# Seven products in place of eight in the first feed-forward product of the last four token blocks

## The chip, the cores and the metric

One core of a Trainium2 chip. The core has five engines with an instruction stream each: PE (TensorE, the matmuls; its weight loads are listed apart as PEld), DVE (VectorE), ACT (ScalarE), POOL (GpSimd) and SP (SyncE, which issues the DMAs here). The metric is the device time of one execution in microseconds; the median of several runs counts.

## The reference

Linear attention with positive random features, whose output goes straight into a feed-forward layer.

```python
# q, k, v: (8 batches, 8 heads, 576 positions, 64); omega: (128, 64)
def phi(x):                          # x is scaled by 64 ** -0.25 before
    h = einsum('bhsd,md->bhsm', x, omega) - sum(x * x, -1, keepdims=True) / 2
    return exp(h - max(h, -1)) / sqrt(128)
num = phi(q) @ (phi(k).T @ v)
den = phi(q) @ sum(phi(k), over positions) + 1e-6
x = (num / den)                      # as (4608 tokens, 512)
h = x @ w_in                         # w_in (512, 2048)
out = gelu(h) @ w_out                # w_out (2048, 512), gelu with erf
```

The matrices `w_in` and `w_out` come as 64-bit floats, which the kernel takes apart itself as 32-bit words. All else is 32-bit.

## The kernel before

**Tiles.** The 4608 tokens are cut into 13 blocks (`TBS`): blocks 0 and 1 of 256 tokens, 2 to 11 of 384, 12 of 256. The 2048 hidden features are cut into 16 chunks of 128. The attention is cut into 32 units: unit k is batch k // 4 and the head pair j = k % 4. Heads 2j and 2j+1 are the 128 rows of x with number j, so a block needs the units of all four j of its batches. Units 0 to 7 run in plain 32-bit arithmetic (`unit_plain`), the others in parts (`split_pre`, `exps_op`, `split_post`). The names at work: `pair`, `shared`, `proj`, `proj_q` (features), `exps` (exponential of a whole unit, one instruction of 2304 columns), `kv` and `kv_split` (features of k times v), `q_trans`, `num`/`num_plain` (numerator and denominator), `den`, `rcp`, `div` (division, which writes x).

**Precision.** From block 1 on a matmul's two operands are each split into a high and a low 16-bit float, after scaling by a power of two, and three products are added in PSUM: high by high, low by high, high by low. So `mm1(n, c, p)` computes a chunk c of h, transposed (128 features by the block's tokens), in 12 matmuls: four pieces of 128 rows of x, three products each, in three steps p. `gelu` works in place in the PSUM bank, `g_high` (ACT) writes the high part, `g_low` (DVE) the low part, and `mm2` multiplies both with the chunk of `w_out` and adds over the chunks in a bank `acc` for every 128 tokens. In block 12 the last 128 tokens go in two halves of 256 columns. `block_high` and `block_low` split x itself, once per block and row piece.

**PSUM.** Eight banks in three rings: `at` (3, the attention), `h` (2, first product), `acc` (3, second product).

**The start.** The weights arrive in 16 pieces (`w_load`), are converted (`w_hi`, `w_lo`, `w_shift`, `w_sign`, `w_round`), their maximum is found (`w_abs` on ACT, L401; `w_max` on DVE), and from it comes the scale for the splitting (`w_high`, `w_low`). Meanwhile units 0 to 7 run, and block 0 in 32-bit arithmetic.

**Order.** The program is not written in the order in which it runs. Every piece of work is an `op` with its engine, an estimated cost, what it reads and writes, and a due time. `Planner.run` simulates the engines and hands out, on each engine, the ready op with the earliest due time. The due times come from tables: `STARTS` (one number a block), `UDUE` (one a division), `OFF` (an offset for each function), and the numbers in `X`. The order on each engine is then fixed in the program. `block(n)` lists the ops of a block, `block_prep` its scales and the splitting of x; `xs_place` says where x of a block lies in SBUF, `batch_v` loads v of a batch.

Of the kernel before, what the change touches and what calls it, by code (L numbers as in the profile page):

```python
# [19 lines left out]
P = 128  # L20
# [12 lines left out]
STARTS = (286.9, 834.1, 550.56, 94.36, 152.04, 442.97, 960.6, 1406.49, 1456.39, 594.17, 474.25, 1641.87, 2052.18, 1177.77)  # L33
UDUE = (-331.2, 545.76, 564.47, 521.85, -788.34, -416.41, -477.91, -798.59, -502.63, -176.28, 509.12, -321.38, 447.22, 1250.34,
# [16 lines left out]
PORT = {'w_shift', 'w_sign', 'w_low', 'q_shift', 'q_max2', 'q_max4', 'q_low', 'v_b', 'k_low', 'kv_d', 'block_low', 'split_om'}
# [170 lines left out]
def favor_attention_ffn(ctx: ExitStack, tc: tile.TileContext, qT, kT, v, omT, w_in, w_out, out):  # L222
# [39 lines left out]
    vt = [cp.tile([P, NV, D + 1], F32, name=f"vt{i}") for i in range(2)]  # L262
# [21 lines left out]
    mp, dp, late, G = [], [], [], {}  # L284
    bufs = dict(at=3, h=2, acc=3, nm=2, cm=2, ct=2, cg=2, zr=2, km=2, kvz=1, qh=1, kvz2=1, qh2=1, dt=1, rt=1, rc=2, mx=1, nq=1, mc=1, kvs=1,
                vsc=2, bs=4, be=2, xs=4, raw=2, r=2 if X['xm'] else 3, lo=2, qt=2, ql=2 if X['qm'] else 4, kvh=1, kvl=1, xh=8, xl=8, g=3, gh=3, gl=3, o=2)
    for k, b in bufs.items():
# [4 lines left out]
                 vsc=(P, 2), bs=(P, 6), be=(32, 1), xs=(P, T), raw=(P, 2048), r=(P, 2 * HS if X['xm'] else HS), lo=(P, 2, M), qt=(P, QW, HS), ql=(P, QW, HS),  # L292
                 kvh=(P, 2, P), kvl=(P, 2, P), xh=(P, T), xl=(P, T), g=(P, T), gh=(P, T), gl=(P, T), o=(P, DM))
    kinds = dict(raw=I32, r=F32R, ql=F32R, kvh=F32R, kvl=F32R, xh=F16, xl=F16, gh=F16, gl=F16)
    pools = dict(raw=dp, r=late, lo=late, qt=late, ql=late, kvh=late, kvl=late, xh=mp, xl=mp, g=mp, gh=mp, gl=mp, o=mp)

    def alloc(name, k):
        if name in ('at', 'h', 'acc'):
            G[k] = pp.tile([P, 512], F32, tag=name, name=name, bufs=bufs[name])
            return  # L300
        if name in ('qh2', 'kvz2'):
            G[k] = qh2 if name == 'qh2' else kvz2
            return
# [197 lines left out]
    for b in range(B):  # L501
        for j in range(NJ):
# [5 lines left out]
            u.v = vt[u.k % 2] if u.kp else vst[:, b % 2, j]  # L508
            u.vk = ('vt', u.k % 2) if u.kp else ('vst', b % 2, j)
# [25 lines left out]
    def load_vst(b):  # L535
        nc.sync.dma_start(vst[:, b % 2].rearrange("p j n d -> p j (n d)"), v[b].rearrange("j p n d -> p j (n d)"))
# [120 lines left out]
    xk, xplace = [0], {}  # L657

    def xs_place(n, j):
        if (n, j) not in xplace:  # L660
            if n < 2:
                xplace[n, j] = (xa[:, j, T0[n]:T0[n + 1]], ('xa', n, j))
            elif n == 2:
                xplace[n, j] = (None, ('xs', n, j))
            else:
                k = NKK + xk[0] % (NF - NKK)
                xk[0] += 1
                xplace[n, j] = (w32f[:, 1, k, 0:T], ('xw', k))
# [16 lines left out]
    started = set()  # L685

    def finish_unit(u, half):
        ps = xs_pieces(u.b, half)
        keys, new = [], []
        for n, c0, c1, r0 in ps:  # L690
            k = xs_place(n, u.j)[1]
            if n == 2 and (n, u.j) not in started:
                new.append(('xs', k))
            else:
                keys.append(k)
            started.add((n, u.j))
        pn = [('pn', u, half, a) for a in range(2)]
        return ps, keys, new, pn

    def out_ops(u, half):  # L700
        ps, keys, new, pn = finish_unit(u, half)
# [5 lines left out]
           new=[(ring, k) for k in pn] + new)  # L707
# [4 lines left out]
        op('DVE', c, div, u, half, due=(2, 2 * u.k + half, 0.0, 0.0), r=pn + [('rt', u, half)], w=keys + [k for _, k in new])  # L712
# [51 lines left out]
    def x_high(u, x):  # L764
        a, b = XR[x]
        nc.scalar.copy(G['r', u, x][:, 0:b - a], xf[:, a:b])  # L766

# [172 lines left out]
    def batch_v(b):  # L940
        us = units[b * NJ:(b + 1) * NJ]
        op('SP', 0, load_vst, b, w=[u.vk for u in us], size=1311e3)
        for u in us:
            op('DVE', 0.8, v_max, u, r=[u.vk], w=[('vm', b)])
        chain(b, 0)
        op('POOL', 0.8, v_scales, b, r=[('exp', b, 0)], new=[('vsc', ('vsc', b))])
        op('ACT', 0.3, v_spread, b, w=[('vsc', b)])

    def split_pre(u):
# [5 lines left out]
        for i in range(NK + 4):  # L955
# [27 lines left out]
        op('DVE', 1.33, q_shift, u, r=[nq], w=qe)  # L983
# [123 lines left out]
    def block_prep(n):  # L1107
# [8 lines left out]
        op('POOL', 0.21, block_out, n, r=[('bs', n), ('wsc', 0)], w=[('bo', n)])  # L1116
        t = TB[n]
# [4 lines left out]
    def ffn_first(n, c):  # L1122
        t = TB[n]
        k = 'F' if n >= N32 else 'F0'
        if n < N32:
# [4 lines left out]
            op('ACT', 0.1 + t / 1000, gelu, n, c, r=[('h', n, c)], new=[('g', ('g', n, c))], tab='g', kind=k)  # L1130
# [22 lines left out]

    def p2():
# [34 lines left out]
    for win in (1, 0):  # L1189
# [6 lines left out]
       w=[('w32', 0, c) for c in range(NF)] + [('e2',)] + [(x, 1, t) for x, n in (('et', NT), ('eq', 4)) for t in range(n)] + [('vst', a, j) for a in range(2) for j in range(NJ)])  # L1196
    op(None, 0, nothing, w=[('w32', 1, c) for c in range(NKK)] + ['kk'] + [('kk', g) for g in range(len(KG))])
    for c in range(NKK, NF):
        op(None, 0, nothing, w=[('w32', 1, c), ('xw', c)])
    done_u = NJ  # L1200
    for n in range(1, NBLK):
        b1 = (T0[n + 1] - 1) // S
        while done_u < (b1 + 1) * NJ:
            u = units[done_u]
            if u.j == 0 and not u.kp:
                batch_v(u.b)
# [12 lines left out]
            if us[-1].j == NJ - 1:  # L1219
                chain(u.b, 1)  # L1220
# [45 lines left out]
```

## Time and profile before

| | us |
|---|---|
| runs, median (lowest to highest of 3) | 991.94 (991.08 to 991.99) |
| span of the profiled execution | 989.5 |
| PE, 0 to 100 us: busy | 83.8 |
| PE, 100 to 150 us: busy | 50.0 of 50 |
| last matmul of the attention (L632) | 850.2 |

The page gives the span of the profiled execution, from its first to its last instruction, and no time of its own for what lies around it; the median of the runs stands 2.4 us above the span. The view by stretch gives the busy time of each engine between two moments. A row of a group reads: line, engine, operation, written tile <- read tiles, shape, count | busy time in us, mean time of one in ns | idle time of the engine before it, and who ended it. A row in order of time reads: start, duration, engine, line, operation, and in brackets the idle time before it. A matmul's recorded time includes its way through the array, during which the next one already streams; its pace is read from the starts.

### The profile page before, as it was taken

How to read it: one execution, taken by the hardware profiler on the slowest of the kernel's cores; microseconds unless marked ns; L12 is line 12 of the kernel's file. 1: busy time of each engine (PE TensorE's matmuls, PEld its weight loads, DVE VectorE, ACT ScalarE, POOL GpSimd, SP SyncE). 2: the span in 40 equal slices, each digit the busy share in tenths (PEclk: the TensorE clock that was granted, in tenths of full speed). 3: DMA queues.
4: the chain of work that ended last, by engine and by line, in shares of the span. 5: the costliest groups of instructions: out<-in, count | busy, mean ns of one | idle time of the engine just before them, and what ended most of it. 6: DMA issues, size and time to landing. Idle time of an engine off the chain costs nothing.

```text
span 989.5 us, 17528 instructions
## 1 busy us (share of the span) xinstructions
PE 966.3 (98%) x5996; PEld 603.3 (61%) x5996; DVE 727.5 (74%) x1947; ACT 734.8 (74%) x1515; POOL 354.2 (36%) x552
## 2 busy tenths in 40 slices
PE   7978999999999999999999999999999999999998
PEld 6666666666656566565656666566655556555576
DVE  4987888888989788888988799878775577421111
ACT  6977859788889869788798878978785677542233
POOL 2233334445347327444453535543431422100000
PEclk7978999999999999999999999999999999999999
DMA  8755322422122032013211132121211100000000
GB/s 254 231 182 160 122 83 70 154 71 62 65 80 73 26 109 73 25 55 100 77 49 60 46 102 81 49 61 45 49 31 51 49 1 33 1 22 12 1 33 22
DMA packets 45992, 70.92 MB, mean 72 GB/s; under 512 B 13392, under 2 KB 21968, under 8 KB 45904
## 3 DMA queue, kind: packets, MB, share of 16 engines
q1 hardware_dynamic: 45904, 69.81, 23.9%
q8 instruction: 48, 0.79, 0.4%
q14 instruction: 40, 0.33, 0.1%
HBM read 60.36 MB, written 9.44 MB: 71 GB/s over the span
## 4 chain that ended last, share of the span: by engine, by line
PE 78%; DVE 11%; ACT 6%; DMA 1%; issue 1%; POOL 1%; SPq 1%; ACTq 0%; DVEq 0%; POOLq 0%
PE h L1058 31%; PE acc L1082 10%; PE acc L1084 9%; PE acc L1083 9%; PE h L1053 3%; PE at L632 3%; PE at L779 2%; PE acc L1079 2%; PE at L801 2%; PE at L880 2%; PE at L575 2%; DVE xl L1047 1%; DVE gl L1074 1%; DMA vt<-in_v 1%; DVE mx L806 1%
## 5 line engine op out<-in xcount | busy, mean ns | idle before, releaser
L771 POOL TENSOR_TENSOR r<-xt,r 64x256 fp32r<-64x256 f32 (+2 forms) x216 | 173.5, 821 | 243.4 <-ACT r L766 163.5
L1058 PE MATMUL h<-xh,wih 128*128 128x384 f16 (+1 forms) x768 | 243.6, 317 | 2.9 <-DVE gl L1074 2.6
L1058 PE MATMUL h<-xl,wih 128*128 128x384 f16 (+1 forms) x768 | 243.8, 317 | 0.0
L1058 PE MATMUL h<-xh,wil 128*128 128x384 f16 (+1 forms) x768 | 243.6, 317 | 0.0
L1082 PE MATMUL acc<-woh,gh 128*128 128x512 f16 (+1 forms) x544 | 205.3, 377 | 0.0
L1084 PE MATMUL acc<-wol,gh 128*128 128x512 f16 (+1 forms) x544 | 204.5, 376 | 0.0
L1083 PE MATMUL acc<-woh,gl 128*128 128x512 f16 (+1 forms) x544 | 204.5, 376 | 0.0
L1074 DVE SCALAR_TENSOR_TENSOR gl<-h,bs,gh 128x384 f16<-128x384 f32 (+1 forms) x192 | 112.5, 589 | 120.4 <-ACT gh L1070 118.9
L1058 PEld LDWEIGHTS <-wih 128*128 128x128 f16 x1536 | 147.1, 98 | 86.0 <-issue 0.7
L1066 ACT ACTIVATE h<-h,bs 128x384 f32<-128x384 f32 (+1 forms) x192 | 102.9, 536 | 92.4 <-PE h L1058 91.0
L1070 ACT ACTIVATE gh<-h,bs 128x384 f16<-128x384 f32 (+1 forms) x192 | 107.5, 562 | 68.8 <-PE acc L1084 56.7
L1058 PEld LDWEIGHTS <-wil 128*128 128x128 f16 x768 | 75.0, 98 | 50.1 <-issue 7.2
L1084 PEld LDWEIGHTS <-gh 128*128 128x128 f16 x560 | 54.8, 98 | 62.6
L766 ACT CAST r<-xt 128x256 fp32r<-128x256 f32 (+2 forms) x216 | 82.7, 409 | 12.4 <-PE at L801 3.4
L1082 PEld LDWEIGHTS <-gh 128*128 128x128 f16 x560 | 54.5, 97 | 48.3 <-issue 0.2
L1083 PEld LDWEIGHTS <-gl 128*128 128x128 f16 x560 | 55.0, 98 | 43.2 <-issue 0.3
L683 DVE TENSOR_TENSOR w<-at,rt 64x128 f32<-64x128 f32 (+6 forms) x168 | 54.6, 325 | 3.7
L779 PE MATMUL at<-om,r 128*128 128x256 f32 x216 | 53.8, 337 | 0.0
L394 POOL TENSOR_TENSOR w<-w 128x1024 int32<-128x1024 int32 x12 | 28.7, 2388 | 65.7 <-DVE w L391 42.0
L643 ACT ACTIVATE dt<-at,vsc 64x288 f32<-64x288 f32 x96 | 47.6, 496 | 4.5 <-PE at L632 2.0
L801 PE MATMUL at<-r,om 128*128 128x288 f32 x192 | 47.4, 337 | 0.0
L648 DVE STREAM_TRANSPOSE rt<-dt 128x288 f32<-128x288 f32 x64 | 30.3, 474 | 21.1 <-ACT dt L643 17.2
(213 smaller groups left out, 1770.7 us busy)
## 6 DMA issues: line engine op xcount, KB each, us to landing
xt<-in_kT SPq DMA_DIRECT2D x56, 288.0 KB, 3.9
xt<-in_qT SPq DMA_DIRECT2D x56, 288.0 KB, 3.8
out_x<-o SPq DMA_DIRECT2D x35, 256.0 KB, 2.0
raw<-in_w_in SPq DMA_DIRECT2D x16, 512.0 KB, 6.3
raw<-in_w_out SPq DMA_DIRECT2D x16, 512.0 KB, 4.5
w<-in_v SPq DMA_DIRECT2D x6, 1280.0 KB, 6.2
vt<-in_v SPq DMA_DIRECT2D x8, 320.0 KB, 5.0
out_x<-o SPq DMA_DIRECT2D x2, 128.0 KB, 1.9
```

The costliest lines, as they stand in the source:

```text
L683: nc.vector.tensor_tensor(x[r, c0:c1], ps[r, r0:r1], rt[r, r0:r1], op=ALU.mult)
L766: nc.scalar.copy(G['r', u, x][:, 0:b - a], xf[:, a:b])
L771: nc.gpsimd.tensor_tensor(r, xf[D:, a:b], r, op=ALU.subtract)
L779: nc.tensor.matmul(o[:, t], r[:, t * P:(t + 1) * P], om, start=True, stop=True)
L801: nc.tensor.matmul(G['pp', u, NK + g][:, 0:HS], om[:, i], xr_part(u, NK + g), start=(i == 0), stop=(i == 1))
L1058: nc.tensor.matmul(h[:, 0:t], w, (G['xh', n, j], G['xh', n, j], G['xl', n, j])[k][:, 0:t], start=(i == 0), stop=(i == 3 * NJ - 1))
L1066: nc.scalar.activation(h, h, AF.Gelu, scale=G['bs', n][:, 2:3])
L1070: nc.scalar.activation(G['gh', n, c][:, 0:t], G['h', n, c][:, 0:t], AF.Copy, scale=G['bs', n][:, 3:4])
L1074: nc.vector.scalar_tensor_tensor(G['gl', n, c][:, 0:t], G['h', n, c][:, 0:t], G['bs', n][:, 3:4], G['gh', n, c][:, 0:t], op0=ALU.mult, op1 ...
L1082: nc.tensor.matmul(acc, gh[:, s], woh[:, c, c0:c1], start=(c == 0), stop=False)
L1083: nc.tensor.matmul(acc, gl[:, s], woh[:, c, c0:c1], start=False, stop=False)
L1084: nc.tensor.matmul(acc, gh[:, s], wol[:, c, c0:c1], start=False, stop=(c == NF - 1))
```

## The change

For blocks 9 to 12 (`is_w`) the first product is done by Strassen's method in Winograd's form. `w_in` transposed is cut into four quarters: chunks 0 to 7 and 8 to 15, rows j = 0, 1 and j = 2, 3 of x. x of a block is cut the same way by rows, and by halves of the tokens. With A for the weights and B for x:

- sums of weights, once: S0 = A21 + A22, S1 = S0 - A11, S2 = A11 - A21, S3 = A12 - S1 (`s_sum`, on POOL; for chunks 0 and 1 later and from the 16-bit parts, `s_sum2`), each split into high and low part (`s_high`, `s_low`);
- sums of x, once per block: T1 = B12 - B11, T2 = B22 - T1, T3 = B22 - B12, T4 = B21 - T2 (`b_sum`, on POOL); the seven operands are split by `b_high`, `b_low`;
- two chunks of each half (a group, `q` = 0 to 3) make seven products of 12 matmuls (`w_prod`), on 192 columns (128 in block 12): P1 = A11 B11, P5 = S0 T1, P6 = S1 T2, P2 = A12 B21, P7 = S2 T3, P3 = S3 B22, P4 = A22 T4.

They share three banks. W collects P1 + P6, then P7, then P4. After P1 ACT copies W into V (`w_seed`), to which P2 is added. After P5, which goes to U, ACT copies U into SBUF as s (`w_snap`). After P6 DVE writes W + s into U (`c_sum`), to which P3 is added; after P7 DVE writes W + s into s. V, U, W and s are then the four quarters of h; `c_gelu`, `c_high` and `c_low` treat each of them, and `w_mm2` is the second product as before. W and U come from the rings `h` or `at`, V from `h`.

Besides: `TOP` is 12 in place of 13; the tables `STARTS`, `UDUE`, `OFF` and several numbers of `X` are new; x lies in eight pairs of row pieces (`pair_at`), the copy of k in parts (`kk`) in the buffers of v; v is loaded unit by unit (`load_vst(u)`); tiles `gh` and `gl` are twice as long and also serve block 0.

```diff
-TOP = 13
+TOP = 12
...
-STARTS = (286.9, 834.1, 550.56, 94.36, 152.04, 442.97, 960.6, 1406.49, 1456.39, 594.17, 474.25, 1641.87, 2052.18, 1177.77)
+STARTS = (-608.76, -310.19, 1013.97, 411.45, 613.3, 691.46, 1509.94, 850.35, 1239.92, 423.8, 1230.35, 1650.1, 1806.11,
...
-    def load_vst(b):
+    def load_vst(u):
+        nc.sync.dma_start(u.v, v[u.b, u.j])
...
+    WHICH = ((1, 0, 0), (5, 3, 3), (6, 2, 2), (2, 1, 1), (7, 4, 4), (3, 6, 6), (4, 5, 5))
+    GP = 2
+
+    def is_w(n):
+        return n >= X['n0']
...
+    def s_sum(c, k):
+        a11, a12, a21, a22 = s_src(c)
+        if k % 2 == 0:
+            x, y, o = (a21, a22, ALU.add) if k == 0 else (a11, a21, ALU.subtract)
+        else:
+            x, y, o = (s_tmp(c, 0), a11, ALU.subtract) if k == 1 else (a12, s_tmp(c, 1), ALU.subtract)
+        nc.gpsimd.tensor_tensor(s_tmp(c, k), x, y, op=o)
...
+    def b_sum(n, i):
+        x, y = {3: (7, 0), 2: (6, 3), 4: (6, 7), 5: (1, 2)}[i]
+        nc.gpsimd.tensor_tensor(b_src(n, i), b_src(n, x), b_src(n, y), op=ALU.subtract)
...
+    BANK = {1: 'W', 6: 'W', 7: 'W', 4: 'W', 2: 'V', 5: 'U', 3: 'U'}
+
+    def w_prod(n, q, p, i, first, last):
+        h, b = TB[n] // 2, G[BANK[p], n, q]
+        xh, xl = b_tile(n, i, 0), b_tile(n, i, 1)
+        k = 0
+        for g in range(GP):
+            for kt in range(2):
+                ah, al = a_side(p, GP * q + g, kt)
+                for w, x in ((ah, xh), (al, xh), (ah, xl)):
+                    nc.tensor.matmul(b[:, g * h:(g + 1) * h], w, x[:, kt], start=first and k == 0, stop=last and k == 6 * GP - 1, skip_group_check=True)
+                    k += 1
...
+    def w_snap(n, q):
+        nc.scalar.copy(flat(n, ('s', n, q)), flat(n, ('U', n, q)))
+
+    def w_seed(n, q):
+        nc.scalar.copy(flat(n, ('V', n, q)), flat(n, ('W', n, q)))
+
+    def c_sum(n, q, to):
+        nc.vector.tensor_tensor(flat(n, to), flat(n, ('W', n, q)), flat(n, ('s', n, q)), op=ALU.add)
...
+    def wino_second(n, q):
+        NI, h = TB[n] // P, TB[n] // 2
+        order = ((0, 0), (1, 2), (1, 0), (1, 1), (0, 1), (0, 2)) if NI == 3 else ((0, 0), (1, 0), (1, 1), (0, 1))
```

The tables move instructions on every engine. Three places follow as the order of the built programs shows them, with the engine, the line and the tiles (numbers are buffers).

ACT at the start, around the exponentials of unit 4 (`et` to `et`, 2304 columns). Before; L401 is `w_abs`, L382 and L385 the conversion of weights, L637 `den`:

```order
L385 ACTIVATE w32_71<-raw_507 128x1024
L401 ACTIVATE w32_71,wmax_75<-w32_71 128x1024 x2
L637 ACTIVATE dt_659<-acc_635 128x288
L401 ACTIVATE w32_71,wmax_75<-w32_71 128x1024 x2
L637 ACTIVATE dt_676<-acc_626 128x288
L382 ACTIVATE raw_618<-raw_618 128x1024
L568 ACTIVATE et_82<-et_82 128x2304
```

and with the change, where the same functions are L408, L424, L660, L405 and L591:

```order
L408 ACTIVATE w32_71<-raw_502 128x1024
L591 ACTIVATE et_81<-et_81 128x2304
L424 ACTIVATE w32_71,wmax_74<-w32_71 128x1024
L660 ACTIVATE dt_671<-at_650 128x288
L424 ACTIVATE w32_71,wmax_74<-w32_71 128x1024
L405 ACTIVATE raw_633<-raw_633 128x1024
```

The exponentials now follow the conversion of piece 5 at once; three of the four maxima and the conversion of piece 6 stand behind them.

DVE in the last group of block 12. Before, the low parts of the last chunks follow one another (L1074):

```order
L1074 SCALAR_TENSOR_TENSOR gl_11725<-h_11677,bs_10692,gh_11719 128x256
L1074 SCALAR_TENSOR_TENSOR gl_11763<-h_11714,bs_10692,gh_11758 128x256
L1074 SCALAR_TENSOR_TENSOR gl_11779<-h_11731,bs_10692,gh_11773 128x256
L1074 SCALAR_TENSOR_TENSOR gl_11817<-h_11768,bs_10692,gh_11812 128x256
L1074 SCALAR_TENSOR_TENSOR gl_11830<-h_11785,bs_10692,gh_11825 128x256
```

and with the change (L1307 is `c_sum`, L1328 `c_low`; h_12422 is W, at_12441 is U, h_12439 is V, and s lies in wil):

```order
L1307 TENSOR_TENSOR at_12441<-h_12422,wil_68 128x256
L1328 SCALAR_TENSOR_TENSOR gl_12513<-h_12439,bs_11089,gh_12499 128x2x128
L1307 TENSOR_TENSOR wil_68<-h_12422,wil_68 128x256
L1328 SCALAR_TENSOR_TENSOR gl_12513<-at_12441,bs_11089,gh_12499 128x2x128
L1328 SCALAR_TENSOR_TENSOR gl_12562<-wil_68,bs_11089,gh_12555 128x2x128
L1328 SCALAR_TENSOR_TENSOR gl_12562<-h_12422,bs_11089,gh_12555 128x2x128
```

Two sums of banks stand between the four low parts of a group, and PE waits for each of them before its next product into the bank.

PE at the last product of the program. Before, the last matmul of chunk 15's `mm1` and what follows:

```order
L1058 MATMUL h_11785<-xl_10932,wih_67 128x256
L1082 LDWEIGHTS gh_11719
L1082 MATMUL acc_11479<-woh_69,gh_11719 128x512
L1083 LDWEIGHTS gl_11725
L1083 MATMUL acc_11479<-woh_69,gl_11725 128x512
```

and with the change the last matmul of P4 and the second product (L1392 to L1394) of the first quarter (gh_12499):

```order
L1294 MATMUL h_12422<-xl_11970,wih_67 128x128
L1392 LDWEIGHTS gh_12499
L1392 MATMUL acc_12108<-woh_69,gh_12499 128x512
L1393 LDWEIGHTS gl_12513
L1393 MATMUL acc_12108<-woh_69,gl_12513 128x512
```

Before, 45 matmuls of five chunks follow the last first product, 36 of them of earlier chunks; now 36 matmuls follow, and the six with gh_12499 stand ahead of the first that needs P4 (with gh_12555).

More of the change, by code (lines that the diff above doesn't have):

```diff
@@ L683, in div @@
                 nc.vector.tensor_tensor(x[r, c0:c1], ps[r, r0:r1], rt[r, r0:r1], op=ALU.mult)
-    started = set()
     def finish_unit(u, half):
         ps = xs_pieces(u.b, half)
[L689 to L698, printed above, removed]
+        return ps, [xs_place(n, u.j)[1] for n, _, _, _ in ps], [('pn', u, half, a) for a in range(2)]
     def out_ops(u, half):
-        ps, keys, new, pn = finish_unit(u, half)
+        ps, keys, pn = finish_unit(u, half)
         qs = (half,) if X['qm'] else (half, 2 + half)
@@ L982, in split_pre @@
         op('POOL', 0.23, q_max6, u, w=[nq])
[L983 removed]
+        if X['qs']:
+            op('POOL', 2.14, q_shift_p, u, r=[nq], w=qe)
+        else:
+            op('DVE', 1.33, q_shift, u, r=[nq], w=qe)
     def exps_op(us):
@@ new lines, in s_scale, with s_high, s_low, sums_of_weights @@
+    def s_scale(c):
+        return 1.0 if c < 2 else wsc[:, 1, 1:2]
+    def s_high(c, k):
+        nc.scalar.activation(s_place(c, k)[0], s_tmp(c, k), AF.Copy, scale=s_scale(c))
+    def s_low(c, k):
+        h, l = s_place(c, k)
+        nc.vector.scalar_tensor_tensor(l, s_tmp(c, k), s_scale(c), h, op0=ALU.mult, op1=ALU.subtract)
+    def sums_of_weights(c):
+        ks = [('w32', 1, c), ('w32', 1, c + NF // 2)]
+        parts = [(x, 1, c + y) for x in ('wh', 'w') for y in (0, NF // 2)]
+        for k in range(4):
+            op('POOL', 0.62 if c > 1 else 0.62 * (3, 2)[k % 2], s_sum if c > 1 else s_sum2, c, k, r=(ks if c > 1 else parts) + ['w0f'] + ([('st', c, k // 2)] if k % 2 else []),
+                   new=[('tx', ('st', c, k))])
+        op(None, 0, nothing, w=ks + [('sw', c)])
+        for k in range(4):
+            op('ACT', 0.4, s_high, c, k, r=[('st', c, k), ('sw', c), ('wsc', 1)], w=[('swh', c, k)], kind='W')
+            op('DVE', 0.42, s_low, c, k, r=[('st', c, k), ('sw', c), ('wsc', 1), ('swh', c, k)], w=[('swl', c, k)], kind='W')
@@ L1154, in p2, with w_mm2 @@
+    def w_mm2(n, q, a, g, i, c0, c1, begin, end):
+        acc, c = G['acc', n, i, c0][:, 0:c1 - c0], chunks(q, a)[g]
+        gh, gl = (G[x, n, q, a][:, g * TB[n] + i * P:g * TB[n] + (i + 1) * P] for x in ('gh', 'gl'))
+        nc.tensor.matmul(acc, gh, woh[:, c, c0:c1], start=begin, stop=False)
+        nc.tensor.matmul(acc, gl, woh[:, c, c0:c1], start=False, stop=False)
+        nc.tensor.matmul(acc, gh, wol[:, c, c0:c1], start=False, stop=end)
+    acc_begun = set()
+    WR = X['wr']
     def p2():
@@ L1205, in favor_attention_ffn @@
             if u.j == 0 and not u.kp:
+                if u.k == X['kvp']:
+                    op(None, 0, nothing, w=[('vt', 0), ('vt', 1), 'kk'] + [('kk', g) for g in range(len(KG))])
                 batch_v(u.b)
```

271 lines of the change are left out of this document (221 added, 50 removed), and 8 rows, old and new, of the table UDUE.

## The prediction

> **What bounds the kernel now.** I read first the page of the profile: the span, the busy times, and the row of PE in 40 slices.
>
> ```profile
> span 989.5 us, 17528 instructions
> ...
> PE 966.3 (98%) x5996; PEld 603.3 (61%) x5996; DVE 727.5 (74%) x1947; ACT 734.8 (74%) x1515; POOL 354.2 (36%) x552
> ...
> PE   7978999999999999999999999999999999999998
> ...
> PEclk7978999999999999999999999999999999999999
> ```
>
> TensorE is busy from the fifth slice to the end, at the full granted clock; only the first 100 us have holes. Second, the busy times by stretch (length, then busy time of PE, PEld, DVE, ACT, POOL), third the list of waits of PE.
>
> ```profile
> 0.00:100.00 100.00, 83.83 (x594) 63.41 (x595) 74.95 (x169) 77.00 (x168) 30.31 (x32) 0.86 0.70 208
> 150.00:850.00 700.00, 697.39 (x4318) 426.40 (x4318) 581.12 (x1650) 571.84 (x1201) 306.29 (x506) 1.00 0.21 62
> 850.00:947.00 97.00, 96.91 (x538) 52.51 (x538) 21.57 (x41) 35.63 (x67) 0.23 (x1) 1.00 0.03 9
> ```
>
> ```profile
> PE at L575 <- ACT et L568: 8.3, 2, 5.8
> PE at L613 <- ACT et L559: 4.0, 1, 4.0
> PE h L1058 <- DVE gl L1074: 2.6, 8, 0.6
> ```
>
> From 150 to 850 us PE idles 700 - 697.39 = 2.6 us, from 850 to 947 us 0.1 us. Of the visible waits 12.3 us lie in two lines of the attention at the start. A busy share alone would not do, since a matmul's recorded time overlaps the next one's; so, fourth, the starts of matmuls in the order of time (start, duration, engine, line, operation).
>
> ```profile
> 902.13 0.33 PE L1058 MATMUL h<-xh,wih 128*128 128x384 f16 x1
> ...
> 906.03 0.38 PE L1082 MATMUL acc<-woh,gh 128*128 128x512 f16 x1
> ...
> 909.91 0.33 PE L1058 MATMUL h<-xh,wih 128*128 128x384 f16 x1
> ```
>
> ```profile
> 960.60 0.27 PE L1058 MATMUL h<-xh,wih 128*128 128x256 f16 x1
> ...
> 963.22 0.38 PE L1082 MATMUL acc<-woh,gh 128*128 128x512 f16 x1
> ```
>
> Between 902.13 and 906.03 stand 24 matmuls of 384 columns: 3.90/24 = 162.5 ns from start to start. Between 906.03 and 909.91 stand 18 of 512: 215.6 ns. Between 960.60 and 963.22 stand 24 of 256: 109.2 ns. Each further 128 columns cost 53.2 ns, so a matmul costs about 2.7 ns + 0.416 ns a column, with a weight load for every one. The stream is without gaps: **after the start the time is the number of streamed columns**, and a column removed there is worth 0.416 ns.
>
> **The change part by part.** *Products.* A block of 384 tokens now has 16 chunks x 12 = 192 matmuls of 384 columns in its first product, 192 x 162.5 ns = 31.20 us. Four groups x seven products x 12 = 336 matmuls of 192 columns take their place; at 2.7 + 80 = 82.6 ns (estimate from the line above) that is 27.75 us, 3.45 us less. The block of 256: 192 x 109.2 ns = 20.97 us against 336 of 128 columns at 55.9 ns = 18.78 us, 2.19 us less. Three blocks and one: 3 x 3.45 + 2.19 = **12.5 us off PE**. The matmuls of the second product keep number and shape (48 groups of three in each of the four blocks).
>
> The 55.9 ns is new ground: no long run of such short matmuls is in the trace. The nearest row is the split of k and v, runs of four with 65, 129, 65 and 129 columns:
>
> ```profile
> 205.86 0.34 PE L880 MATMUL at<-vb,w 128*128 128x65 f16 x4
> 206.03 0.33 PE L1058 MATMUL h<-xh,wih 128*128 128x384 f16 x1
> ```
>
> Four matmuls with four weight loads in 0.17 us; the line gives 4 x 2.7 + 388 x 0.416 = 172 ns. So the load does not set the pace even at 65 columns, in a run of four. From the other side, the shortest pace kept up over 24 is the 109.2 ns above. I take 55.9, nearest to the run of short ones, and keep 109.2 for a rival.
>
> On this point the Trainium skill (TensorE: Matmul & The Clock Gate, "Back-to-back issue gap") speaks against the change: in a sustained stream of weight load and matmul it gives about 81 ns per matmul of 128 columns, where the columns alone would take 56. By it the last block's products cost 336 x 25.1 ns = 8.4 us more, and the sum below would be 988.0. The same sentence gives 131 ns for 512 columns, where the rows above show 215.6; no run here shows its figure for 128.
>
> *Work added off PE.* It has these rows as prices (group, count, busy time, mean ns):
>
> ```profile
> L1070 ACT ACTIVATE gh<-h,bs 128x256 f16<-128x256 f32 x32 | 15.2, 474 | 14.9 <-PE at L1084 9.8 <-PE acc L1084 4.8
> L1066 ACT ACTIVATE h<-h,bs 128x256 f32<-128x256 f32 x32 | 14.3, 448 | 16.0 <-PE h L1058 15.9
> L1066 ACT ACTIVATE h<-h,bs 128x384 f32<-128x384 f32 x160 | 88.5, 553 | 76.5 <-PE h L1058 75.2 <-DVE w L683 0.4
> L1043 ACT ACTIVATE xh<-w,bs 128x384 f16<-128x384 f32 x36 | 20.0, 604 | 0.7 <-DVE w L683 0.5
> L1074 DVE SCALAR_TENSOR_TENSOR gl<-h,bs,gh 128x384 f16<-128x384 f32 x160 | 97.2, 611 | 84.3 <-ACT gh L1070 83.0
> L1074 DVE SCALAR_TENSOR_TENSOR gl<-h,bs,gh 128x256 f16<-128x256 f32 x32 | 15.4, 480 | 36.1 <-ACT gh L1070 35.9
> L1047 DVE SCALAR_TENSOR_TENSOR xl<-w,bs,xh 128x384 f16<-128x384 f32 x36 | 23.7, 697 | 2.1 <-POOL bs L309 1.2 <-ACT xh L1043 0.8
> L771 POOL TENSOR_TENSOR r<-xt,r 64x256 fp32r<-64x256 f32 x96 | 74.3, 789 | 140.1 <-ACT r L766 90.2 <-issue 23.7 <-PE at L779 11.9
> ```
>
> ACT gets 32 high parts of weight sums (32 x 0.474 = 15.2 us), 32 copies of banks (24 x 0.553 + 8 x 0.474 = 17.1) and 12 more operands (9 x 0.604 + 3 x 0.474 = 6.9): 39 us. DVE gets 32 low parts (15.4), 32 sums of banks (24 x 0.611 + 8 x 0.480 = 18.5) and 12 operands (9 x 0.697 + 3 x 0.480 = 7.7): 42 us. POOL gets 60 sums; at 0.789 us for 256 columns the 44 of the weights cost 35 us and the 16 of up to 384 at most 16 x 1.18 = 19, against 700 - 306 = 394 us idle. What must fit before 850 us, where the attention still runs, is the weight sums and two blocks, some 29 us of DVE and 27 of ACT; the second row by stretch shows 700 - 581.12 = 119 us idle on DVE and 128 on ACT there, while PE waited 2.6 us in all. I cost it at nothing: it fills idle time beside a PE that has its own work. Without that cover it would be up to 29 us. The loads of v come in 24 pieces instead of 6, which adds 18 issues to a queue that nothing waited for.
>
> *Waits added.* A group's seven products share three banks, and between them stand hand-offs: ACT copies the first product into a second bank and the fifth out of the third, DVE adds twice. The waiting PE instruction would have the rest of the stream behind it. The order puts at least one whole product (12 x 82.6 = 0.99 us) between a sum's source and its user, mostly a product and six matmuls of the second product (2.3 us); a hand-off needs PE's result (about 0.2 us after the last start, since a recorded matmul of 256 columns lasts 0.27 us and the next starts after 0.11) and one 0.48 to 0.61 us operation, 0.8 us if the engine is free. The present chain of three operations per chunk waited eight times, 2.6 us in all 192 chunks, at most 0.6 us. Bounds: 0, and 0.35 us at each of the 32 sums, 11.2 us. I take 1.7, near the present rate. **Tail:** after the last product stand six matmuls that do not need it (6 x 0.2156 = 1.29 us), where 36 did after the last chunk's first product; the chain to be hidden is 0.2 us, gelu 0.45, high part 0.47 and low part 0.48 with hops, about 1.7 us, and one more matmul (0.22) needs only the high part. That leaves 0.2 us, with the copy queue ahead 0.5. Hand-offs and tail: +2.2.
>
> *Order at the start.* The same instructions run in the first 150 us, in another order. The largest wait of PE stands there (start, duration, and in brackets the idle time before):
>
> ```profile
> 52.74 1.19 PE L623 MATMUL h<-w 128*64 128x288 f32 x8
> 59.73 4.21 PE L575 MATMUL at<-vt,et 128*128 128x65 f32 x18 [5.79 <-ACT et L568]
> ```
>
> ```profile
> 55.20 1.06 ACT L401 ACTIVATE w<-w 128x1024 f32<-128x1024 f32 x1 [1.21 <-POOL w L394]
> 56.17 0.19 ACT L401 ACTIVATION_READ_ACCUMULATOR w<-w 128x1 f32 x1
> 56.26 0.39 ACT L637 ACTIVATE dt<-acc 128x288 f32<-128x288 f32 x1
> 56.55 1.12 ACT L382 ACTIVATE raw<-raw 128x1024 f32<-128x1024 f32 x1
> 57.55 2.12 ACT L568 ACTIVATE et<-et 128x2304 f32<-128x2304 f32 x1
> ```
>
> The exponentials of unit 4 stood behind four maxima of weights (about 1.0 us each, one of them waiting 1.21 us for POOL) and a conversion; the new order puts them ahead of all but one of these, three to five us earlier, and those of unit 5 (the other 2.5 us of the 8.3) ahead of the preparation of block 1. What is late next is the division of unit 3, which now has unit 4's and 5's work ahead of it on DVE. Bounds: all 8.3 us won, or as much as the longest wait, 5.8 us, lost elsewhere in the same 100 us. I take -2.0, nearer to the gain since the longest wait's cause is moved.
>
> **The sum** is made on the profiled span, 989.5 us, and what lies around it; the median of the runs shown, 991.94 us, stands 2.4 us above the span, and I leave that as it is. 991.9 - 12.5 + 2.2 - 2.0 = **979.6 us**.
>
> **The rivals.** (a) *The start wins both waits*: -8.3 in place of -2.0, 973.3 us. For it: the two causes are moved; against it: the decode of the weights behind them remains. (b) *The start loses* 5.8 us: 991.9 - 12.5 + 2.2 + 5.8 = 987.4. (c) *A new wait takes the saving's place*: every one of the 32 sums stops PE for 0.35 us, with DVE still full of attention: 991.9 - 12.5 + 11.2 + 0.5 = 991.1, no change. Against it: two of the four blocks run after 850 us, where DVE is busy 22 of 97 us. (d) *The other side: pairs of weight load and matmul have a floor c of their own* in long runs, which the queue hides in runs of four. It acts in the 1344 matmuls of the products; the loss is 336 x (c - 55.9) ns from 56 on, and 1008 x (c - 82.6) ns more from 83 on. It eats the 12.5 us at c = 85, and at 90 ns it is 19 us: 998.6 us, slower. The rows bound c by 43 ns (the run of four) and 109 ns. (e) *The same floor at 80 ns*: only the last block pays, 336 x 24.1 = 8.1 us: 987.7. The 81 ns of the Trainium skill is this case.
>
> **How the numbers follow.** The forecast's own case, between 975 and 985, has 0.56; (a) 0.12, (b) 0.10, (c) 0.08, (d) 0.06, (e) 0.08. Predicted is 979.6. The range takes in (a), (b) and (e) and leaves out (c) and (d), 0.14: 972 to 989. Faster or slower count from 0.2% (2 us), about what a measurement of this kernel can tell from no change: faster 0.56 + 0.12 + 0.10 + 0.08 = 0.86, same 0.08, slower 0.06.
>
> **What would show it.** The product line of blocks 9 to 11 starting every 82 to 83 ns, that of block 12 every 56; at 80 or more in the last, (d) or (e). PE's waits on the two bank sums and copies under 2 us in all; 10 or more is (c). PE idle in the first 100 us at 14 us in place of 16.2. PE idle from 150 to 850 us still near 3 us; if it is 10 or more, the added work of DVE and ACT had no cover. The prediction is wrong if the stage from 150 us on does not shrink by 10 to 13 us.

## The result, and the profile after

The changed kernel takes 984.68 us (median of 4 runs, 984.07 to 985.51) where the kernel before took 991.51 (4 runs, 991.03 to 991.99): ratio 0.9932, 95% interval 0.9918 to 0.9946, so 6.8 us faster. Forecast were 979.6 us, in a range of 972 to 989, and a gain of 12.3.

The page of the changed kernel, with the rows that were shown of before:

```profile
span 982.9 us, 18957 instructions
...
PE 951.7 (97%) x6572; PEld 625.3 (64%) x6572; DVE 768.7 (78%) x2023; ACT 764.7 (78%) x1591; POOL 419.5 (43%) x612
...
PE   7988999899999999999999999999999999999998
...
PEclk7999999999999999999999999999999999999999
```

PE is busy 14.6 us less than before while the span is only 6.6 us shorter; the difference, 8.0 us, is new idle time. The row of tenths is too coarse for it. The busy times by stretch (length, then busy time of PE, PEld, DVE, ACT, POOL, then granted clock) show the place; the first row is of the kernel before, the others of the changed one:

```profile
150.00:400.00 250.00, 249.36 (x1582) 156.51 (x1582) 220.70 (x638) 213.70 (x459) 119.67 (x191) 1.00 0.27 77
```

```profile
0.00:100.00 100.00, 85.31 (x620) 61.66 (x621) 79.89 (x177) 83.98 (x178) 35.43 (x33) 0.93 0.70 212
150.00:400.00 250.00, 240.33 (x1499) 149.68 (x1498) 232.24 (x643) 216.77 (x474) 161.22 (x232) 1.00 0.26 74
150.00:850.00 700.00, 686.90 (x4487) 435.44 (x4486) 597.85 (x1666) 580.37 (x1226) 355.86 (x541) 1.00 0.21 61
850.00:947.00 97.00, 97.00 (x823) 68.86 (x821) 36.50 (x67) 49.08 (x96) 9.20 (x21) 1.00 0.05 17
```

From 150 to 850 us PE idles 13.1 us where it idled 2.6, and 9.7 of them lie between 150 and 400 us, where no product of the new kind has begun; before it was 0.6 there. The list of PE's waits in the changed kernel (total, times, longest) names the line:

```profile
PE h L1081 <- DVE gl L1097: 7.6, 10, 1.7
...
PE at L793 <- POOL r L785: 2.0, 2, 1.8
...
PE h L1294 <- DVE at L1307: 0.7, 1, 0.7
```

The ordinary first products (L1081, `mm1`) wait for a bank `h` that `g_low` (L1097) has to read empty. One such wait in the order of time, with DVE's rows, then POOL's, then PE's (start, duration, in brackets the idle time before):

```profile
185.10 2.33 DVE L1232 SCALAR_TENSOR_TENSOR w<-w,wsc 128x256 f16<-128x256 f32 x1
187.35 0.47 DVE L818 STREAM_TRANSPOSE et<-at 128x288 f32<-128x288 f32 x1
187.86 0.45 DVE L820 TENSOR_REDUCE mx<-et 128x9 f32<-128x288 f32 x1
188.23 0.48 DVE L1097 SCALAR_TENSOR_TENSOR gl<-h,bs,gh 128x256 f16<-128x256 f32 x1
```

```profile
184.84 2.31 POOL L811 TENSOR_TENSOR et<-et,nm 128x1152 f32<-128x1152 f32 x1
```

```profile
186.67 0.38 PE L1107 MATMUL acc<-wol,gh 128*128 128x512 f16 x1
188.76 0.27 PE L1081 MATMUL h<-xh,wih 128*128 128x256 f16 x1 [1.71 <-DVE gl L1097]
```

L1232 is `s_low`, the low part of a sum of weights. It takes 2.33 us and ends 0.28 us after POOL's shift of the features (`k_shift`, L811); three instructions later comes the `g_low` for which PE has stood still 1.71 us. Groups of these sums (busy time, mean ns): two of `s_low` on DVE, and the largest of `s_sum` on POOL:

```profile
L1232 DVE SCALAR_TENSOR_TENSOR w<-w,wsc 128x256 f16<-128x256 f32 x18 | 12.5, 706 | 0.0
L1232 DVE SCALAR_TENSOR_TENSOR w<-xa,wsc,w 128x256 f16<-128x256 f32 x6 | 5.8, 964 | 0.0
L1206 POOL TENSOR_TENSOR w<-w 128x256 f32<-128x256 f32 x18 | 14.2, 797 | 9.6 <-DVE w L1232 8.4 <-DVE vexp L938 0.6
```

The forecast had priced a low part at 0.48 us from a row whose source lies in PSUM; 24 of the 32 take 0.76 us on the mean (18.3 us).

### The profile page after: what moved, and what is told of

Its sections match the earlier page's. It is cut to its first block, busy times and chain, and to the rows that moved or that the text cites. A ratio compares the mean times of both kernels' runs of the same rounds, so it can differ in the third digit from the quotient of the medians.

```text
span 982.9 us, 18957 instructions
## 1 busy us (share of the span) xinstructions
PE 951.7 (97%) x6572; PEld 625.3 (64%) x6572; DVE 768.7 (78%) x2023; ACT 764.7 (78%) x1591; POOL 419.5 (43%) x612
## 4 chain that ended last, share of the span: by engine, by line
PE 68%; DVE 18%; ACT 5%; POOL 3%; issue 2%; DMA 1%; SPq 1%; ACTq 0%; POOLq 0%
PE h L1081 16%; PE h L1294 5%; PE acc L1105 5%; PE acc L1107 5%; PE acc L1106 5%; PE at L1294 5%; PE acc L1393 4%; PE acc L1394 4%; PE acc L1392 4%; PE acc L1102 3%; PE at L655 3%; PE h L1076 2%; DVE gl L1097 2%; PE at L793 2%; PE at L897 2%
## 5 line engine op out<-in xcount | busy, mean ns | idle before, releaser
L785 POOL TENSOR_TENSOR r<-xt,r 64x288 fp32r<-64x288 f32 (+2 forms) x216 | 178.2, 843 | 147.0 <-ACT r L776 107.1
L1081 PE MATMUL h<-xh,wih 128*128 128x384 f16 (+1 forms) x512 | 163.7, 320 | 8.3 <-DVE gl L1097 7.6
L1081 PE MATMUL h<-xl,wih 128*128 128x384 f16 (+1 forms) x512 | 163.7, 320 | 0.0
L1081 PE MATMUL h<-xh,wil 128*128 128x384 f16 (+1 forms) x512 | 163.7, 320 | 0.0
L1105 PE MATMUL acc<-woh,gh 128*128 128x512 f16 x368 | 140.2, 381 | 0.0
L1107 PE MATMUL acc<-wol,gh 128*128 128x512 f16 x368 | 139.5, 379 | 0.0
L1106 PE MATMUL acc<-woh,gl 128*128 128x512 f16 x368 | 139.5, 379 | 0.0
L1081 PEld LDWEIGHTS <-wih 128*128 128x128 f16 x1024 | 97.6, 98 | 55.2 <-issue 0.2
L1097 DVE SCALAR_TENSOR_TENSOR gl<-h,bs,gh 128x384 f16<-128x384 f32 (+1 forms) x128 | 75.6, 590 | 24.9 <-ACT gh L1093 23.5
L1093 ACT ACTIVATE gh<-h,bs 128x384 f16<-128x384 f32 (+1 forms) x128 | 72.3, 566 | 13.1 <-PE acc L1107 9.8
L1081 PEld LDWEIGHTS <-wil 128*128 128x128 f16 x512 | 50.0, 98 | 39.2 <-issue 11.8
L1393 PE MATMUL acc<-woh,gl 128*128 128x512 f16 (+1 forms) x192 | 69.4, 361 | 0.1
L1392 PE MATMUL acc<-woh,gh 128*128 128x512 f16 (+1 forms) x192 | 69.4, 362 | 0.0
L1394 PE MATMUL acc<-wol,gh 128*128 128x512 f16 (+1 forms) x192 | 69.4, 361 | 0.0
```

The costliest lines, as they stand in the source:

```text
L785: nc.gpsimd.tensor_tensor(r, xf[D:, a:b], r, op=ALU.subtract)
L1081: nc.tensor.matmul(h[:, 0:t], w, (G['xh', n, j], G['xh', n, j], G['xl', n, j])[k][:, 0:t], start=(i == 0), stop=(i == 3 * NJ - 1))
L1097: nc.vector.scalar_tensor_tensor(G['gl', n, c][:, 0:t], G['h', n, c][:, 0:t], G['bs', n][:, 3:4], G['gh', n, c][:, 0:t], op0=ALU.mult, op1 ...
L1105: nc.tensor.matmul(acc, gh[:, s], woh[:, c, c0:c1], start=(c == 0), stop=False)
L1106: nc.tensor.matmul(acc, gl[:, s], woh[:, c, c0:c1], start=False, stop=False)
L1107: nc.tensor.matmul(acc, gh[:, s], wol[:, c, c0:c1], start=False, stop=(c == NF - 1))
```

## The experiments

All runs stand beside runs of the kernel before on the same chip, whose median was 990.97 to 991.32 us in the four groups. "Against after" is the difference of medians to a1_after, the changed kernel run again (984.40); e1 to e4 ran as one group, x1, e7, e5 and e6 as the next, a1, f1 and f2 as the third, x2 alone. Since most rows are so compared across groups, a difference under 1 us is not read.

| run | what differs | median us (lowest to highest) | ratio to before, 95% | against after | PE idle 150-400 / 400-700 us |
|---|---|---|---|---|---|
| a1_after | nothing | 984.40 (983.81 to 985.12) | 0.992 to 0.9948 | 0 | 9.5 / 0.8 |
| e1_no_sums | no sums of weights | 973.06 (971.87 to 973.93) | 0.98 to 0.9855 | -11.3 | 1.2 / 0.8 |
| e2_no_low | no low parts (DVE) | 977.42 (977.16 to 977.56) | 0.9853 to 0.9897 | -7.0 | 4.1 / 0.6 |
| e3_no_pool | no sums on POOL | 980.54 (980.41 to 982.18) | 0.9887 to 0.9934 | -3.9 | 5.6 / 0.7 |
| e4_no_high | no high parts (ACT) | 986.00 (983.88 to 987.91) | 0.9941 to 0.9967 | +1.6 | 9.5 / 1.4 |
| e7_one_input | low part replaced by a maximum | 979.82 (977.78 to 980.43) | 0.9864 to 0.9894 | -4.6 | 5.7 / 0.7 |
| f1_split | POOL's shift in four pieces | 983.67 (981.72 to 984.53) | 0.9911 to 0.9939 | -0.7 | 7.4 / 1.2 |
| f2_pool | low parts on POOL | 995.95 (995.48 to 996.79) | 1.0037 to 1.0064 | +11.6 | 17.1 / 1.0 |
| x1_later | sums held back to 400 us | 993.30 (991.95 to 995.23) | 1.001 to 1.0028 | +8.9 | 1.2 / 14.0 |
| x2_look | e2 and 32 maxima after 400 us | 982.12 (981.28 to 983.42) | 0.9899 to 0.9932 | -2.3 | 4.1 / 4.3 |
| e5_no_seven | new order, no seven products | 1017.25 (1016.73 to 1017.89) | 1.0241 to 1.0276 | +32.9 | 14.2 / 9.6 |
| e6_before_filled | before, PE's long wait filled | 988.72 (988.13 to 989.41) | 0.9965 to 0.9985 | | 0.6 / 1.6 |

**Which part of the sums costs.** The order on each engine is fixed in the program, so a function can be emptied without moving anything else:

```diff
     def s_low(c, k):
+        return
         h, l = s_place(c, k)
```

and likewise `s_high`, or `s_sum` and `s_sum2`, or all four; where an operand would never be written, `a_side` takes the quarter A11 for it.

> All work on sums of weights (s_sum, s_sum2, s_high, s_low) is left out: the functions issue nothing, and the seven products read quarter A11 in their place; every other instruction keeps its place on its engine. Load theory (the added work on DVE and POOL delays the banks of the ordinary blocks between 150 and 400 us): PE idle from 150 to 850 us falls from 13 us to 3 or 4, time 975 +- 1.5 us. Order theory (the new tables make the waits by themselves): idle stays at 11 to 13 us, time 984 to 985.

> Only the low parts of the sums of weights on DVE (s_low, 32 instructions, 21.6 us of busy time) are left out, the products read low parts of A11. If DVE's added load is the cause, nearly all comes back: PE idle from 150 to 850 us 4 us, time 976. If it is the sums on POOL (shared way to SBUF, x_low later), a third or less comes back: idle 10, time 982. Order theory: idle 12 to 13, time 984.5.

> Only the sums of weights on POOL (s_sum, s_sum2, 48 instructions, about 34 us with the 16-bit ones) are left out; high and low parts are taken of what lies there. If DVE's added load is the cause: PE idle 150 to 850 us 10 to 12 us, time 983. If POOL is the cause, by holding up DVE's instructions with two inputs in SBUF or by coming late with x_low: the mean of s_low falls from 0.68 to about 0.48 us, idle to 5 or 6, time 977 to 978. Order theory: no change.

> Only the high parts on ACT (s_high, 32 instructions, 15.6 us) are left out, the low parts and products read high parts of A11. Load on DVE, POOL, and order: all expect no more than 1 us, 984. Only if ACT's added load delays g_high, and with it g_low, does it fall to 978.

Without any sums the stretch is as full as before the change. Its row in e1_no_sums:

```profile
150.00:400.00 250.00, 248.82 (x1564) 156.57 (x1563) 222.68 (x643) 215.86 (x468) 134.17 (x206) 1.00 0.27 77
```

So the new order by itself makes no idle time in this stretch; the sums do, and they cost 11.3 us, a little more than the load theory had (975 +- 1.5 us was expected). PE idle from 150 to 850 us falls by 8.6 us, to 4.5, so the idle time does not show all of the price. PE's instructions stand in the same order in both kernels, so one can be followed from kernel to kernel. Here is the same one in a1_after and then in e1_no_sums:

```profile
400.13 0.47 PE L793 MATMUL at<-om,r 128*128 128x256 f32 x2
```

```profile
389.82 0.47 PE L793 MATMUL at<-om,r 128*128 128x256 f32 x2
```

At 150 us e1_no_sums was still 0.7 us behind a1_after; here it is 10.3 us ahead, and 10.2 at 850 us. The whole price of the sums, 11.0 us by this count, is therefore paid between 150 and 400 us. What the idle time misses lies in waits short enough to be hidden by the recorded time of a matmul, which outlasts its pace: that is the likely reason, and it was not tested. The low parts alone bring 7.0 us, nearer to the load theory's 976 us than to 982; the sums on POOL bring 3.9, together 10.9; the high parts on ACT nothing (e4 is 1.6 us slower, against a spread of 4 us of its runs). The expectation for e3_no_pool held in the time only by half and failed in its reason: `s_low` did not become shorter. Its group there:

```profile
L1234 DVE SCALAR_TENSOR_TENSOR w<-w,wsc 128x256 f16<-128x256 f32 x18 | 14.0, 790 | 0.0
```

The longest `s_low` there still takes 2.33 us. It is therefore the attention's own work on POOL that `s_low` stands behind, not the new sums.

**Whether DVE's instructions cost, or their standing behind POOL.**

```diff
     def s_low(c, k):
-        nc.vector.scalar_tensor_tensor(l, s_tmp(c, k), s_scale(c), h, op0=ALU.mult, op1=ALU.subtract)
+        nc.vector.tensor_reduce(wcm[:, 0:1], G['st', c, k][:, 0:2 * P], axis=AX.X, op=ALU.max)
```

> The low parts of the sums of weights are replaced, at the same place, by a maximum over the same 256 columns on DVE, with one input in SBUF in place of two; its result is not used, the products read low parts of A11. Only the recorded 2.3 us cases, in which s_low ends together with an instruction of POOL, should go. If the time that DVE stands behind POOL is what costs: mean of the replacement 0.40 to 0.45 us, time near that without low parts, 977.5 to 979. If the mere instructions (32 x 0.44 = 14 us) cost: 981 to 983. If the mean stays at 0.65 or more, one input is held up just the same and the run tells nothing of it.

The view of the replacement's line in e7_one_input (shortest, median and longest duration in ns, first and last start):

```profile
L1232 DVE TENSOR_REDUCE wcm<-w x24: 377/409/420, 185.0 to 348.4; 128x1 f32<-128x256 f32 x24
```

It is never held up: 409 ns at the median, 420 at most. At the same 32 places 13 us of DVE work cost 2.4 us against e2_no_low, and `s_low` 7.0: the time came out between the two expectations. The other 4.6 us go with what is different: the second input, the wait for ACT's high part, which the replacement does not have, and the 256 columns written. To see what the second input does, f1_split shortens what holds `s_low` up:

```diff
     def k_shift(u):
-        es = u.et[:, 0:NT]
-        nc.gpsimd.tensor_tensor(es, es, ...)
+        for a, b in ((0, 2), (2, 4), (4, 6), (6, NT)):
+            es = u.et[:, a:b]
+            nc.gpsimd.tensor_tensor(es, es, ...)
```

> The changed kernel with POOL's shift of the features (k_shift, 128x1152, 2.1 to 2.2 us) issued as four instructions of 256, 256, 256 and 384 columns at the same place. If s_low stands behind one POOL instruction until its end: no s_low of more than about 1.0 us, its mean falls from 0.68 to 0.50 to 0.58, and a third to two thirds of the 4.9 us that one input instead of two brought comes back: 981 to 983. If it stands behind POOL until POOL has no work left: mean and time unchanged, 984.5; POOL's own start cost of three more instructions in each of 24 units may cost up to 1 us.

The same view of `s_low`'s line, of the changed kernel and then of f1_split:

```profile
L1232 DVE SCALAR_TENSOR_TENSOR w<-w,wsc x18: 443/476/2327, 185.1 to 336.9; 128x256 f16<-128x256 f32 x18
```

```profile
L1233 DVE SCALAR_TENSOR_TENSOR w<-w,wsc x18: 444/476/1017, 185.2 to 335.2; 128x256 f16<-128x256 f32 x18
```

The longest falls from 2.33 to 1.02 us when POOL's shift is cut (its pieces of 256 columns take 0.61 us at the median, the whole took 2.11), so `s_low` stands behind one instruction on POOL until its end: that mechanism is shown. The Trainium skill (SBUF — State Buffer, "Who interferes with whom") says that a DVE instruction with two inputs in SBUF contends with a GpSimd instruction that reads SBUF, that the port pair they share is an exclusive lock, and that a DVE instruction with one SBUF input (outside the modes that use both ports) does not contend. These rows, and the 420 ns of the one-input replacement, agree with it. The time, though, fell by 0.7 us only, and the spreads overlap: the expected time of 981 to 983 us did not come, and how much of the 4.6 us is this hold stays open.

**Whether idle time on an engine covers work.** Two runs do the same sums elsewhere. x1_later holds all 96 operations back and lets them out, in their order, one every 3 us:

```diff
+    held, step = [], [400.0]
     def put(o):
+        if o.fn in (s_sum, s_sum2, s_high, s_low):
+            held.append(o)
+            return
+        put_now(o)
+        while held and o.t >= step[0]:
+            step[0] += 3.0
+            put_now(held.pop(0))
```

f2_pool lets POOL subtract (`nc.gpsimd.tensor_tensor(l, s_tmp(c, k), h, op=ALU.subtract)`), after one more scaling on ACT for 24 of the 32.

> The same work on sums of weights, all of it done, but held back and let out one operation every 3 us from about 400 to 690 us, where DVE has 46 us idle in 300 in place of 18 in 250; all other instructions keep their order. Load theory (place, not work, is what costs): PE idle from 150 to 850 us 4 to 6 us, time 975 to 977. If the work itself costs PE wherever it stands (its hold on the way to SBUF): the idle moves to 400 to 690 us, time 982 to 985.

> The changed kernel with the low parts of the sums of weights moved from DVE to POOL at the same place (one subtraction each), after one more scaling on ACT for 24 of them. If a sum's instructions cost by the engine that has them, DVE's 7.3 us go and POOL's 32 instructions (about 24 us) cost as the sums on POOL did, 4 us: 981 to 982. If DVE then stands behind POOL with its other instructions of two inputs, nothing is won: 984 or more.

x1_later came out above both of its expectations, and f2_pool far beyond "nothing is won". The stretch of 400 to 700 us in x1_later, then that of 150 to 400 us in f2_pool and the group of its low parts on POOL:

```profile
400.00:700.00 300.00, 286.02 (x1735) 170.17 (x1733) 259.00 (x708) 245.41 (x517) 172.44 (x252) 1.00 0.23 64
```

```profile
150.00:400.00 250.00, 232.91 (x1430) 142.04 (x1429) 209.24 (x572) 217.88 (x471) 172.82 (x256) 0.99 0.24 71
```

```profile
L1234 POOL TENSOR_TENSOR w<-w 128x256 f16<-128x256 f32 x24 | 19.1, 800 | 4.0 <-ACT w L1230 1.6 <-ACT kvs L904 1.5
```

In x1_later the idle time moves along and grows: PE waits 14.0 us while DVE idles 41 us and POOL 128. In f2_pool DVE is busy 23 us less than in the changed kernel, POOL idles 77 us, and PE idles 17.1 us. PE's waits in that stretch of f2_pool name POOL beside `g_low`; L785 takes the attention's own low parts of q and k (total, times, longest):

```profile
PE h L1081 <- DVE gl L1097: 9.2, 10, 3.0
PE at L815 <- POOL r L785: 4.0, 5, 1.3
PE at L793 <- POOL r L785: 1.9, 2, 1.0
```

In the changed kernel the first is 5.7 us there, and the waits for L785 are 1.8 us. The 24 scalings that f2_pool adds on ACT were not priced apart. So in these two runs neither a lightly used stretch nor a lightly used engine is cover. x2_look takes the sums on POOL and the second input out of x1_later's question:

```diff
+    def look(c):
+        nc.vector.tensor_reduce(wcm[:, 0:1], woh[:, c].bitcast(F32), axis=AX.X, op=ALU.max)
```

> The kernel without low parts of the sums of weights (e2_no_low; the products read low parts of A11), with 32 maxima over 256 columns on DVE added, one every 9 us from about 400 to 690 us, at places where the order has nothing for them; they have one input and nobody uses their result. In e7_one_input the same 32 instructions, 13 us, stood where the order had a slot for them (180 to 360 us) and cost 2.4 us against e2_no_low. If a slot in the order is what counts: 7 to 11 us, time 985 to 988, and PE idle 7 us or more from 400 to 700 us. If DVE's idle time there (45 of 300 us) covers them: 0 to 3 us, 977 to 980; then what made x1_later slow were its sums on POOL.

Its stretch of 400 to 700 us, and the group of the added instructions:

```profile
400.00:700.00 300.00, 295.71 (x1816) 178.83 (x1816) 258.93 (x751) 245.61 (x512) 143.85 (x219) 1.00 0.23 67
```

```profile
L1502 DVE TENSOR_REDUCE wcm<-woh 128x1 f32<-128x256 f32 x32 | 12.8, 401 | 0.0
```

12.8 us of short instructions on DVE cost 4.7 us against e2_no_low, between the two expectations: less than what a missing slot was to cost, more than idle time would let through, and twice what 13 us cost where the order has a place for them (2.4 us in e7_one_input). The rest of what x1_later lost must lie in its sums on POOL, its high parts or the second input; it was not separated.

**The start.** e6_before_filled puts matmuls nobody uses into the longest wait of the kernel before:

```diff
     def kv(u):
+        if u.k == 4:
+            for _ in range(24):
+                nc.tensor.matmul(G['pk', u][:, 256:384], ident, ident, start=True, stop=True, skip_group_check=True)
```

> The kernel before with 24 matmuls more, of the identity into unused columns of the bank, ahead of the product of features and v of unit 4, so that PE is busy in the 5.8 us in which it waits for the exponentials; nothing else changes. If the low granted clock after that wait (0.50 from 60 to 65 us, 0.76 from 65 to 70) is caused by the idle PE and costs time: the clock stays at 1.00 there and the time falls by 2 to 4 us, to 987 to 989. If the clock does not cost (ACT and DVE set the pace there): no change, 991.

The stretches after that wait, of the kernel before and then of e6_before_filled (the clock is the third figure from the end):

```profile
55.00:60.00 5.00, 0.27 (x2) 0.28 (x2) 4.90 (x15) 4.80 (x6) 0.32 (x2) 0.72 0.68 212
60.00:65.00 5.00, 5.00 (x24) 5.00 (x25) 3.45 (x11) 3.91 (x8) 2.36 (x1) 0.50 0.00 0
65.00:70.00 5.00, 5.00 (x32) 3.98 (x31) 3.12 (x6) 3.04 (x6) 1.48 (x2) 0.76 0.87 275
```

```profile
55.00:60.00 5.00, 3.41 (x30) 3.44 (x31) 4.83 (x16) 4.20 (x5) 0.92 (x2) 1.00 0.77 254
60.00:65.00 5.00, 5.00 (x47) 5.00 (x46) 3.78 (x12) 4.75 (x9) 2.38 (x1) 1.00 0.00 0
65.00:70.00 5.00, 5.00 (x40) 3.76 (x39) 4.52 (x8) 2.78 (x6) 3.00 (x2) 1.00 0.87 270
```

This expectation held. After standing still for 5.8 us PE gets half its clock, and from 60 to 70 us it loses about 5.00 x 0.50 + 5.00 x 0.24 = 3.7 us of work by that (an estimate from these rows). Kept busy, it keeps the clock, and the kernel is 2.4 us faster though nothing uses the result of the 24 matmuls. The kernel before shows the same link between its executions: a mean clock of 0.986 goes with spans of 988.5 to 990.7 us, and 0.991, in four of them, with 985.2 to 985.8.

> The order and numbers of the changed kernel with the number of the first seven-product block set to 13, so that no block is done by seven products and no sums of weights are made; the first 1545 rows of PE are those of the changed kernel. If the new order at the start is worth what the profile shows: PE's granted clock 0.97 from 50 to 100 us in place of 0.83, idle there 1.5 us less, 150 us reached 4 to 5 us earlier, and a time of 987 to 989 with an idle of 3 to 6 us from 150 us on. If the start gives nothing: 991 or more.

This expectation failed in the time, 1017.25 us where 987 to 989 was expected, and in one premise: the sums of weights are still made in e5_no_seven. Its time says little, since the tables were not made for these blocks: PE idles 25.6 us from 150 to 850. Its first 100 us are those of the changed kernel, 43.69 us of PE work from 50 to 100 us at a clock of 0.97, so the start does not hang on the seven products.

## Why the prediction was right in sign and too high in gain

- **Products, -12.5 us: right.** The changed kernel's starts in blocks 9 to 11, and in block 12:

```profile
927.19 0.25 PE L1294 MATMUL h<-xh,wih 128*128 128x192 f16 x1
...
928.18 0.38 PE L1392 MATMUL acc<-woh,gh 128*128 128x512 f16 x1
```

```profile
959.41 0.22 PE L1294 MATMUL h<-xh,wih 128*128 128x128 f16 x1
...
960.08 0.27 PE L1392 MATMUL acc<-woh,gh 128*128 128x256 f16 x1
```

  Twelve matmuls of 192 columns take 0.99 us, 82.5 ns each, and twelve of 128 take 0.67, 55.8 ns each; 82.6 and 55.9 were forecast, so the 12.5 us, counts times pace, stand. Rivals (d) and (e), a floor of 90 or 80 ns, fall. The 81 ns for 128 columns of the Trainium skill (TensorE: Matmul & The Clock Gate, "Back-to-back issue gap") does not hold here: over runs of twelve with a weight load each, and over two runs of 24, the trace has 55.8.
- **Hand-offs and tail, +2.2 us: too dear.** PE waits once for a sum of banks, 0.7 us in all. Rival (c) falls. ("A queue that nothing waited for" was not quite so: PE waited 0.9 us for one load of v before and 0.9 after; the 18 further issues show no cost.)
- **Start, -2.0 us: right in sign, too small.** PE idles 14.7 us in the first 100 us where it idled 16.2 (14 was forecast). But most of the gain is the clock, which the step did not count: 0.97 from 50 to 100 us in place of 0.83. The two dips of before after waits (3.7 us of lost work from 60 to 70 us, and from 85 to 95 us 2.50 x 0.21 + 5.00 x 0.48 = 2.9) shrink to one, as these rows of before and of the changed kernel show:

```profile
85.00:90.00 5.00, 2.50 (x14) 2.50 (x14) 3.79 (x8) 4.99 (x6) 2.37 (x1) 0.79 0.01 2
90.00:95.00 5.00, 5.00 (x18) 3.94 (x18) 3.60 (x6) 4.55 (x10) 0.00 (x0) 0.52 0.45 97
```

```profile
75.00:80.00 5.00, 2.53 (x6) 1.19 (x7) 4.64 (x14) 2.29 (x4) 3.88 (x7) 0.88 0.60 211
80.00:85.00 5.00, 5.00 (x18) 2.11 (x16) 3.88 (x5) 3.79 (x7) 4.59 (x5) 0.78 0.00 0
```

  That leaves 2.53 x 0.12 + 5.00 x 0.22 = 1.4 us, 5.2 less. With the 1.5 us of idle time the start is worth 6.7 us, an estimate from these rows. A second, rougher estimate agrees with its size: if each matmul counts as long as the median distance from its form's start to the next start after 100 us, PE has begun 100.0 us of work by 150 us in the kernel before, 105.6 in the changed one and 106.0 in e5_no_seven, so 5.6 to 6.0 us more. e6_before_filled shows 2.4 us of gain from the first dip by an edit of its own; no run has the whole new start in the kernel before. Rival (b), a loss at the start, falls; the size is nearer to rival (a)'s 8.3 us than to 2.0, but through the clock more than through the waits.
- **Added work, "I cost it at nothing: it fills idle time beside a PE that has its own work": this is the step that failed.** The forecast itself said that 10 us or more of idle time from 150 to 850 us would mean that this work had no cover; it is 13.1. e1_no_sums puts the price of the sums of weights at 11.3 us, 7.0 of it the low parts on DVE and 3.9 the sums on POOL. Two things were wrong. The price of a low part was taken from a row with its source in PSUM (0.48 us), and the instruction with both inputs in SBUF stands behind POOL. And the 119 us in which DVE idled were no store of free time. Only 29.3 of them lay between 150 and 400 us, where the work was put, and the runs that put it elsewhere lost more. DVE stands between PE's first products and the two banks they need back, and what stands ahead of a `g_low` delays PE.
- The terms as measured: -12.5 + 0.7 - 6.7 (start: 5.2 of clock and 1.5 of idle time) + 11.3 = -7.2 us, beside the 6.8 between the medians. Two errors of opposite sign, in the start and in the added work, partly hide each other, and that is luck: with the start at the forecast's -2.0 and the other terms as measured the time would have been 991.9 - 12.5 + 0.7 - 2.0 + 11.3 = 989.4 us, outside the forecast's range.
- **The forecast's own last sign of being wrong came out.** It asked that the stage from 150 us on shrink by 10 to 13 us. It went from 989.5 - 150 = 839.5 us to 982.9 - 150 = 832.9, so 6.6 less, and part of even that is work that the new start had done before 150 us. Products, hand-offs and sums of weights together come to -12.5 + 0.7 + 11.3 = -0.5 us: by these estimates nearly all of the measured gain comes from the order at the start, and the seven products, as ordered here, about pay for their own sums. The sign was right, but not for the reason that the forecast gave most weight.

## What to carry over

A share of idle time says whether an engine is the bound, not whether it can take more work: ask which waited-for result stands behind the place where the new instruction goes, and price it there with the operands it really has. Where work is fixed in an order, emptying one function and leaving the order alone prices that work cleanly. A long wait on PE can cost more than its length: here the clock fell to 0.50 after one of 5.8 us. A forecast's own signs of being wrong are to be read even when the number comes out near: here they showed that two terms had changed places.

## What was not expected of the hardware

DVE's instruction with two inputs in SBUF took 443 to 476 ns mostly and up to 2.33 us behind a POOL instruction of 2.31 us; with one input, in e7_one_input, it took 420 ns at most. In the kernel before PE's granted clock went to 0.50 after a wait of 5.8 us; it was 0.50 from 60 to 65 us and 0.76 from 65 to 70, while the work had begun again at 59.7. Moving 32 instructions of about 0.8 us from DVE to POOL, which then still idled a third of the stretch, cost 11.6 us, with 24 more scalings on ACT.
